# Retention and two expert layers on one core: the masks of a chunk's scores taken in the slot that computes the scores

## The chip, the cores and the metric

The kernel runs on one core of a Trainium2 chip. The metric is the device time in microseconds (us). The kernel before takes 1189.74 us, the median of three runs (1189.67 to 1189.8). The execution that the profiler recorded took 1187.96 us, 1.8 us below that median.

## The reference

A retention layer (a linear attention whose state decays by a factor per head) is followed by two feed-forward layers over 3072 tokens, d_model 512 and d_ff 2048:

```python
for t in range(S):                                   # B, H, S, D = 4, 8, 768, 64
    state = gamma * state + k[t] v[t]^T
    y[t] = scale * q[t] @ state
h = x @ w_in;  g = h - tanh(h);  x = g @ w_out       # first layer
h = x @ w_in;  g = elu(h);       x = g @ w_out       # second layer
```

The arithmetic is fp32. The kernel splits operands of its large products into a high and a low part and takes three matmuls for each product.

## The kernel before, in words

**Retention by chunks.** Each of the four sequences is cut into six chunks of 128 tokens; a step s is one chunk of one sequence (24 steps, s = 4 * chunk + sequence). For a step, TensorE (PE) computes the scores of k against q (`att_scores`, 16 records on line 164, into two PSUM banks). VectorE (DVE) multiplies both banks with a table of decays and causal zeros, which gives `pt` (line 173, two instructions: the masks), and from step 4 on multiplies q in place with a table (`att_scale_q`, line 135), which must come after the scores have read q. PE then computes the step's output (`att_out`: line 187 from the scaled q and the state, line 195 from `pt` and v) and, except in the last chunk, what the chunk adds to the state (`att_state`, line 214, from `kn`, which `att_scale_k`, line 149, has scaled on VectorE). One slot later ScalarE (ACT) copies the output into x as its high part (line 203), VectorE makes the low part (line 204), and two small VectorE instructions update the state (lines 237 and 240). The output and the first scores bank share the tag a0, the state's sum and the second scores bank share a1, so the scores of the next step wait for lines 204 and 240.

**Feed-forward by slots.** The main loop runs over slots n = 0 to 191, each one block of 512 tokens by 128 columns of d_ff. In slot n PE runs `first_mm(n)` (12 matmuls, line 251, into one of two h banks), then what `events` has for the slot, then `second_mm(n-2)` (12 matmuls, line 317, into acc). In the first layer the activation g = h - tanh(h) takes four ScalarE instructions (lines 271 to 275) and a chain of four on VectorE (lines 277, 280, 283, 284), and VectorE also makes the low part of the former slot's g (line 264).

**Weights.** They come in as 64-bit words and are converted: ScalarE writes `w32` (line 86, in the slot before), VectorE fixes the bits (lines 93 and 94), and one slot later ScalarE makes the high part (line 106) and VectorE the low one (line 107). Two weight tiles per slot are converted in slots 0 to 4, one in slots 5 to 22, none after. `w32` has four buffers, so line 86 waits until line 107 has read an older one, and ScalarE's queue stands behind it.

**Order.** Everything is under `tc.manual_schedule()`: each engine runs its instructions in the order in which the program emits them. `interleave(chain, side)` emits the activation's chain and a list of side work in turn. `events` puts the scores of steps 5 to 7 into slots 1, 3 and 5, of steps 8 to 11 into slots 22, 24, 26 and 28, and of steps 12 to 23 into slots 33 to 77; output and state of a step are in the slot after its scores. What a generator does after its `yield` runs at the head of the next slot (`for g in gens: run(g)`). `scale_k` puts line 149 at the end of the scores' slot.

Of the kernel before, what the change touches and what calls it, by code (L numbers as in the profile page):

```python
# [14 lines left out]
ALU = mybir.AluOpType  # L15
# [25 lines left out]
def retention_moe_kernel(ctx: ExitStack, tc: tile.TileContext, dims, ins, out):  # L41
    nc = tc.nc
    B, H, S, D, DM, DFF = dims
# [23 lines left out]
    dtab = const.tile([P, 2, NP, P], F32, name="dtab")  # L67
# [10 lines left out]
    def fetch(m, f):  # L78

        raw[m, f] = wp.tile([P, TB], I64, tag=f"w{m % 2}_{f}", name=f"raw{m}_{f}")  # L80
        nc.sync.dma_start(out=raw[m, f], in_=ins[f"w{m}"][f])

    def convert_a(job):

        w = w32[job] = stg.tile([P, TB], F32, tag="w32", name=f"w32_{job[0]}_{job[1]}")
        nc.scalar.activation(out=w, in_=raw[job].bitcast(F32)[:, 1::2], func=AF.Prelu, scale=REBIAS, alpha=NEG)

    def convert_b(job):

        r, w = raw[job].bitcast(U32), w32[job]  # L90
        wu = w.bitcast(U32)
        return [
            lambda: nc.vector.tensor_single_scalar(wu, wu, 3, op=ALU.logical_shift_left),
            lambda: nc.vector.scalar_tensor_tensor(
                out=wu, in0=r[:, 0::2], scalar=29, in1=wu,
                op0=ALU.logical_shift_right, op1=ALU.bitwise_or,
            ),
        ]

    def convert_c(job):  # L100

        m, f = job
        w = w32.pop(job)
        del raw[job]
        t = wts[job] = wp.tile([P, 2, TB], F32R, tag=f"w{m % 2}_{f}", name=f"w{m}_{f}")
        nc.scalar.activation(out=t[:, 0, :], in_=w, func=AF.Copy)  # L106
        return lambda: nc.vector.tensor_tensor(
            out=t[:, 1, :], in0=w, in1=t[:, 0, :].bitcast(F32), op=ALU.subtract
        )
# [7 lines left out]
    def bank(s, part):  # L117

        tag = {"sc0": "a0", "sc1": "a1", "o": "a0"}[part]
        if s < B:  # L120
            tag = [("a0", "a1", "acc0"), ("acc1", "acc2", "acc3")][s % 2][("sc0", "sc1", "o").index(part)]
        return ps_acc if tag[:3] == "acc" else ps_a, tag
# [5 lines left out]
    def att_load_v(s):  # L128
        v = att.tile([P, TB], F32, tag="v", bufs=B, name=f"v{s}")
        nc.sync.dma_start(out=v, in_=ins["qkv"][s][:, 2, :])  # L130
        qkv_t[s][1] = v

    def att_scale_q(s):
        q = qkv_t[s][0][:, 0, :].rearrange("p (a i) -> p a i", a=NP)
        nc.vector.tensor_tensor(out=q, in0=q, in1=qtab, op=ALU.mult)  # L135

    def att_load_kn(s, kn=None):
        if s // B == NCH - 1:
            return
        if kn is None:  # L140
            kn = att.tile([P, TB], F32, tag="kn", name=f"kn{s}")
        nc.sync.dma_start(out=kn, in_=ins["qkv"][s][:, 3, :])
        qkv_t[s][2] = kn

    def att_scale_k(s):
        if s // B == NCH - 1:
            return
        k = qkv_t[s][2].rearrange("p (h d) -> p h d", h=H)
        nc.vector.tensor_tensor(out=k, in0=k, in1=ktab.to_broadcast([P, H, D]), op=ALU.mult)  # L149

    def att_scores(s):
        t = qkv_t[s][0]
        if s < B:
            pt = tmp.tile([P, 2, NP, P], F32, tag="g", bufs=G_BUFS, name=f"pt{s}")
        else:
            pt = att1.tile([P, 2, NP, P], F32, tag="pt", name=f"pt{s}")
        sc = []
        for j in range(2):
            pool, tag = bank(s, f"sc{j}")
            sc.append(pool.tile([P, NP, P], F32, tag=tag, name=f"sc{s}_{j}"))  # L160
        for p in range(NP):
            for j in range(2):
                r = slice(j * D, (j + 1) * D)
                nc.tensor.matmul(
                    out=sc[j][:, p, :],
                    lhsT=t[r, 1, p * P:(p + 1) * P],
                    rhs=t[r, 0, p * P:(p + 1) * P],
                    start=True, stop=True,
                )
        pt_t[s] = pt  # L170
        yield
        for j in range(2):
            nc.vector.tensor_tensor(out=pt[:, j], in0=sc[j], in1=dtab[:, j], op=ALU.mult)  # L173
        if s >= B:
            att_scale_q(s)

    def att_out(s):
        t, v, _ = qkv_t[s]
# [66 lines left out]
    def first_mm(m, x, f, n):  # L245
        h = ps_h.tile([P, TB], F32, tag="h", name=f"h{m}_{n}")
        w = wts[m, f]
        i = 0
        for c in range(KC):
            for a, b in ((0, 0), (0, 1), (1, 0)):  # L250
                nc.tensor.matmul(  # L251
                    out=h, lhsT=w[:, a, c * P:(c + 1) * P], rhs=x[:, b, c, :],
                    start=(i == 0), stop=(i == 3 * KC - 1),
                )
                i += 1
        return h
# [6 lines left out]
    def split_lo(t, g):  # L263
        nc.vector.tensor_tensor(out=t[:, 1, :], in0=g, in1=t[:, 0, :].bitcast(F32), op=ALU.subtract)  # L264
# [107 lines left out]
    def run(g):  # L372
        for _ in g:
            pass
# [4 lines left out]
    with tc.manual_schedule():  # L379
# [36 lines left out]
        g_sc, g_out = {}, {}  # L416

        def scores_pe(s):
            g_sc[s] = att_scores(s)
            next(g_sc[s])  # L420
# [5 lines left out]
        def interleave_into(dst, lists):  # L426
            while any(lists):
                for ops in lists:
                    if ops:
                        dst.append(ops.pop(0))  # L430

        def ops(lst):
            for op in lst:
                op()
# [37 lines left out]
            run(g)  # L472
        att_load_v(B)
        att_load_kn(B)
        scores_pe(B)
        ops(convert_b(jobs0[2]))
        run(g_sc[B])
        att_scale_k(B)
        ops(convert_b(jobs0[3]))

# [15 lines left out]
        def interleave(*lists):  # L496
            while any(lists):
                for ops in lists:
                    if ops:
                        ops.pop(0)()  # L500
# [20 lines left out]
        def load_step(s):  # L521
            att_load(s, att.tile([P, 2, TB], F32, tag="qk", name=f"qk{s}"))
            att_load_kn(s)
# [6 lines left out]
        gens = []  # L530
# [6 lines left out]
        def second(upto):  # L537
            while len(pend) > upto:
                pm, pf, pn, pb, lo, hi = pend.pop(0)
                second_mm(pm, pf, pn, lo, hi)  # L540
                if pb == NB - 1 and pm == 1:
                    fetch(3, pf)
                if pf == NF - 1 and pm == 1 and pb == 0:
                    finish_rest(pb)
                elif pf == NF - 1:
                    finish(pm, pb)
                elif pf == hi - 1:
                    finish_part(pb)
# [5 lines left out]
        for ph, b, f, flo, fhi in order:  # L554
            first, last = b == 0, b == NB - 1
            for g in gens:
                run(g)
            if n < NF:
                for job in jobs0[12 + 2 * n:14 + 2 * n]:
                    fetch(*job)  # L560
            jobs = todo.get(n, [])
            h = first_mm(2 * ph, xhl[ph * NB + b], f, n)
            gens = []
            for g, *args in events.get(n, []):
                gens.append(g(*args))
                next(gens[-1], None)
            v, chain = (act_elu if ph else act_tanhshrink)(h, n, flush)
            halves = [convert_c(job) for job in prev_jobs]
            side = []
            interleave_into(side, [convert_b(j) for j in jobs])  # L570
            side += halves
            if prev_v is not None:
                side.insert(0, lambda: split_lo(g_t[n - 1], prev_v))
            interleave(chain, side)
            if n in scale_k:
                att_scale_k(scale_k[n])
            for job in todo.get(n + 1, []):
                convert_a(job)
            prev_v = v
            prev_jobs = jobs  # L580
            pend.append((2 * ph + 1, f, n, b, flo, fhi))
            if ph == 0 and last:
                fetch(2, f)
            second(SKEW)

            if n in load:
                load_step(load[n])
            if n in load_v:
                att_load_v(load_v[n])
            nxt = 0 if ph == 0 and last else b + 1 if ph else None  # L590
            if nxt is not None and nxt < NB:
                if f == 6:
                    load_x1(nxt)
                if 8 <= f < 8 + KC:
                    split_x1(nxt, f - 8)
            n += 1
# [63 lines left out]
```

## Time and profile before

| | |
|---|---|
| median of three runs | 1189.74 us |
| the profiled execution, and its span | 1187.96 us, 1186.2 us |
| PE busy | 1152.7 us, 97% of the span |
| PE weight loads busy | 943.5 us, 80% |
| VectorE busy | 682.8 us, 58% |
| ScalarE busy | 624.0 us, 53% |
| mean granted TensorE clock | 0.993 |
| chain that ended last | PE 83%, VectorE 8%, issue 4%, ScalarE 2%, DMA 2% |

A busy share is a mean over stages: VectorE's tenths in the page's 40 slices are 7 to 8 over most of the first sixth of the span and 3 to 4 in the second half. An idle time stands with the engine that waited, and what ended it with the engine that was waited for.

### The profile page before, as it was taken

How to read it: one execution, taken by the hardware profiler on the slowest of the kernel's cores; microseconds unless marked ns; L12 is line 12 of the kernel's file. 1: busy time of each engine (PE TensorE's matmuls, PEld its weight loads, DVE VectorE, ACT ScalarE, POOL GpSimd, SP SyncE). 2: the span in 40 equal slices, each digit the busy share in tenths (PEclk: the TensorE clock that was granted, in tenths of full speed). 3: DMA queues.
4: the chain of work that ended last, by engine and by line, in shares of the span. 5: the costliest groups of instructions: out<-in, count | busy, mean ns of one | idle time of the engine just before them, and what ended most of it. 6: DMA issues, size and time to landing. Idle time of an engine off the chain costs nothing.

```text
span 1186.2 us, 15678 instructions
## 1 busy us (share of the span) xinstructions
PE 1152.7 (97%) x6038; PEld 943.5 (80%) x6039; DVE 682.8 (58%) x1133; ACT 624.0 (53%) x1097; POOL 5.6 (0%) x10
## 2 busy tenths in 40 slices
PE   7799999999999999999999999999999999999998
PEld 5577887787888887888888888888888888888886
DVE  4877887656665666666689766334343333333332
ACT  2456775454445454544678766444544444453534
POOL 0000000100000000000000000000000000000000
PEclk8899999999999999999999999999999999999999
DMA  9750030513103100200476400200200200200000
GB/s 355 296 227 19 18 107 27 116 36 71 53 19 107 36 28 1 89 28 1 145 229 196 141 1 1 71 1 1 72 1 1 72 1 1 72 1 1 36 1 36
DMA packets 27562, 80.44 MB, mean 68 GB/s; under 512 B 3168, under 2 KB 3168, under 8 KB 27488
## 3 DMA queue, kind: packets, MB, share of 16 engines
q1 hardware_dynamic: 26048, 76.56, 18.6%
q0 software_dynamic: 864, 2.10, 1.2%
q8 instruction: 47, 0.77, 0.3%
q10 hardware_dynamic: 576, 0.79, 0.2%
q14 instruction: 27, 0.22, 0.1%
HBM read 64.76 MB, written 14.68 MB: 67 GB/s over the span
## 4 chain that ended last, share of the span: by engine, by line
PE 83%; DVE 8%; issue 4%; ACT 2%; DMA 2%; ACTq 0%; DVEq 0%; SPq 0%
PE acc L317 41%; PE h L251 38%; PE o L187 2%; PE o L195 2%; DVE pt L173 2%; DVE v L284 1%; DVE kn L149 1%; ACT v L272 1%; DVE v L280 1%; DVE qk L135 1%; DVE h L283 1%; DMA kn<-qkv 1%; ACT u L271 1%; DMA raw<-w 1%; DMA gtab<-gtab 1%
## 5 line engine op out<-in xcount | busy, mean ns | idle before, releaser
L317 PE MATMUL acc<-g,w 128*128 128x512 f32 x1152 | 281.8, 393 | 0.0
L251 PE MATMUL h<-x,w 128*128 128x512 f32 x1152 | 277.7, 390 | 0.0
L317 PE MATMUL acc<-w,g 128*128 128x512 f32 x1152 | 276.7, 389 | 0.6 <-DVE g L264 0.6
L251 PE MATMUL h<-y,w 128*128 128x512 f32 x1152 | 276.7, 389 | 0.0
L317 PEld LDWEIGHTS acc<-w,g 128*128 128x128 f32 x1152 | 216.2, 188 | 45.8 <-DVE g L264 1.0
L251 PEld LDWEIGHTS h<-x,w 128*128 128x128 f32 x1152 | 216.5, 188 | 45.3 <-ACT w L106 0.2
L251 PEld LDWEIGHTS h<-y,w 128*128 128x128 f32 x1152 | 216.3, 188 | 44.8
L317 PEld LDWEIGHTS acc<-g,w 128*128 128x128 f32 x1152 | 213.4, 188 | 47.0 <-ACT g L260 0.7
L297 DVE SCALAR_TENSOR_TENSOR v<-v,t 128x512 f32<-128x512 f32 x96 | 66.5, 693 | 299.6 <-ACT t L295 299.6
L292 ACT ACTIVATE u<-h 128x512 f32<-128x512 f32 x96 | 57.4, 598 | 259.8 <-PE h L251 258.3
L271 ACT ACTIVATE u<-h 128x512 f32<-128x512 f32 x96 | 57.4, 598 | 245.8 <-issue 214.5
L277 DVE SCALAR_TENSOR_TENSOR v<-v,u 128x512 f32<-128x512 f32 x96 | 66.4, 692 | 161.4 <-ACT v L272 161.3
L264 DVE TENSOR_TENSOR g<-v,g 128x512 fp32r<-128x512 f32 x192 | 131.5, 685 | 0.8 <-ACT g L260 0.8
L260 ACT ACTIVATE g<-v 128x512 fp32r<-128x512 f32 x192 | 118.1, 615 | 2.0 <-DVE v L300 2.0
L284 DVE COPY_PREDICATED v<-m,h 128x512 f32<-128x512 uint16 x96 | 70.7, 736 | 6.0
L272 ACT ACTIVATE v<-u,qa_b 128x512 f32<-128x512 f32 x96 | 69.5, 724 | 3.2
L275 ACT ACTIVATE m<-u,xs_b 128x512 bf16<-128x512 f32 x96 | 68.2, 710 | 0.0
L283 DVE TENSOR_TENSOR h<-h,t 128x512 f32<-128x512 f32 x96 | 66.5, 693 | 0.0
L300 DVE TENSOR_TENSOR v<-h,v 128x512 f32<-128x512 f32 x96 | 65.7, 684 | 0.0
L280 DVE SCALAR_TENSOR_TENSOR v<-v,h 128x512 f32<-128x512 f32 x96 | 65.3, 681 | 0.0
L293 ACT ACTIVATE v<-u 128x512 f32<-128x512 f32 x96 | 60.6, 631 | 3.1
L295 ACT ACTIVATE t<-u 128x512 f32<-128x512 f32 x96 | 59.2, 617 | 0.0
(44 smaller groups left out, 605.2 us busy)
## 6 DMA issues: line engine op xcount, KB each, us to landing
raw<-w SPq DMA_DIRECT2D x64, 512.0 KB, 5.4
qk<-qkv SPq DMA_DIRECT2D x20, 512.0 KB, 4.7
v<-qkv SPq DMA_DIRECT2D x24, 256.0 KB, 6.1
x<-x1d SPq DMA_DIRECT2D x12, 512.0 KB, 5.8
kn<-qkv SPq DMA_DIRECT2D x20, 256.0 KB, 5.6
out<-o SPq DMA_DIRECT2D x10, 512.0 KB, 2.9
x1d<-o SPq DMA_DIRECT2D x8, 512.0 KB, 3.4
stage<-qkv SPq DMA_DIRECT2D x4, 512.0 KB, 6.8
```

What stands on the lines that cost most here:

```text
L251: nc.tensor.matmul(out=h, lhsT=w[:, a, c * P:(c + 1) * P], rhs=x[:, b, c, :], start=(i == 0), stop=(i == 3 * KC - 1),)
L260: nc.scalar.activation(out=t[:, 0, :], in_=g, func=AF.Copy)
L264: nc.vector.tensor_tensor(out=t[:, 1, :], in0=g, in1=t[:, 0, :].bitcast(F32), op=ALU.subtract)
L271: nc.scalar.activation(out=u, in_=h, func=AF.Square)
L272: nc.scalar.activation(out=v, in_=u, func=AF.Square, bias=qa_b)
L275: nc.scalar.activation(out=big, in_=u, func=AF.Relu, bias=xs_b)
L277: lambda: nc.vector.scalar_tensor_tensor(out=v, in0=v, scalar=QB, in1=u, op0=ALU.add, op1=ALU.mult),
L280: lambda: nc.vector.scalar_tensor_tensor(out=v, in0=v, scalar=C2, in1=h, op0=ALU.mult, op1=ALU.mult),
L283: lambda: nc.vector.tensor_tensor(out=h, in0=h, in1=th, op=ALU.subtract),
L284: lambda: nc.vector.copy_predicated(out=v, mask=big.bitcast(U16), data=h),
L297: lambda: nc.vector.scalar_tensor_tensor(out=v, in0=v, scalar=1.0, in1=th, op0=ALU.add, op1=ALU.mult),
L317: nc.tensor.matmul(out=acc[e], lhsT=lhsT, rhs=rhs, start=(f == lo and i == 0), stop=(f == hi - 1 and i == 2),)
```

## The change

The masks and the scaling of q of step 5 and later are no longer run at the head of the slot after the scores. `att_scores` hands them out as three functions at its `yield`; the main loop puts them into the side list of the scores' own slot, behind its first entry, so that they alternate with the activation's chain. Steps 0 to 3 keep their order, and step 4's is the same as before.

```diff
         pt_t[s] = pt
-        yield
-        for j in range(2):
-            nc.vector.tensor_tensor(out=pt[:, j], in0=sc[j], in1=dtab[:, j], op=ALU.mult)
-        if s >= B:
-            att_scale_q(s)
+        masks = [
+            lambda j=j: nc.vector.tensor_tensor(out=pt[:, j], in0=sc[j], in1=dtab[:, j], op=ALU.mult)
+            for j in range(2)
+        ]
+        if s < B:
+            yield
+            for op in masks:
+                op()
+        else:
+            yield masks + [lambda: att_scale_q(s)]
...
             gens = []
+            masks = []
             for g, *args in events.get(n, []):
                 gens.append(g(*args))
-                next(gens[-1], None)
+                masks += next(gens[-1], None) or []
...
             if prev_v is not None:
                 side.insert(0, lambda: split_lo(g_t[n - 1], prev_v))
+            side[1:1] = masks
             interleave(chain, side)
```

Only VectorE's order changes; that of PE, ScalarE, SyncE and GpSimd is the same. In the rows below `v` and `h` are the activation's chain, `w` the weights, `pt` the masks' results, `sc` the scores, `qk` the scaling of q and `kn` that of k. Line numbers of the changed kernel are up to five higher, and the masks' line is 172.

VectorE in slot 1 (scores of step 5), from behind line 280 of the chain, before:

```order
L93 TENSOR_SCALAR w_0_4_433<-w_0_4_433 128x512
L283 TENSOR_TENSOR h_1_447<-h_1_447,t_472 128x512
L93 TENSOR_SCALAR w_1_2_435<-w_1_2_435 128x512
L284 COPY_PREDICATED v_473<-m_474,h_1_447 128x512
L94 SCALAR_TENSOR_TENSOR w_0_4_433<-raw_4_155,w_0_4_433 128x512
L94 SCALAR_TENSOR_TENSOR w_1_2_435<-raw_2_157,w_1_2_435 128x512
L107 TENSOR_TENSOR w_3_481<-w_0_3_359,w_3_481 128x512
L107 TENSOR_TENSOR w_1_483<-w_1_1_361,w_1_483 128x512
L149 TENSOR_TENSOR kn_365<-kn_365,ktab 128x512
L173 TENSOR_TENSOR pt_460<-sc_0_461,dtab 128x512
L173 TENSOR_TENSOR pt_460<-sc_1_462,dtab 128x512
L135 TENSOR_TENSOR qk_363<-qk_363,qtab 128x512
```

and now:

```order
L172 TENSOR_TENSOR pt_460<-sc_0_461,dtab 128x512
L288 TENSOR_TENSOR h_1_447<-h_1_447,t_472 128x512
L172 TENSOR_TENSOR pt_460<-sc_1_462,dtab 128x512
L289 COPY_PREDICATED v_473<-m_474,h_1_447 128x512
L135 TENSOR_TENSOR qk_363<-qk_363,qtab 128x512
L93 TENSOR_SCALAR w_0_4_433<-w_0_4_433 128x512
L93 TENSOR_SCALAR w_1_2_435<-w_1_2_435 128x512
L94 SCALAR_TENSOR_TENSOR w_0_4_433<-raw_4_155,w_0_4_433 128x512
L94 SCALAR_TENSOR_TENSOR w_1_2_435<-raw_2_157,w_1_2_435 128x512
L107 TENSOR_TENSOR w_3_481<-w_0_3_359,w_3_481 128x512
L107 TENSOR_TENSOR w_1_483<-w_1_1_361,w_1_483 128x512
L149 TENSOR_TENSOR kn_365<-kn_365,ktab 128x512
```

The three instructions move ahead of six instructions on weights and of the scaling of k, which all come three places later.

VectorE in slot 24 (scores of step 9, no weights any more), before:

```order
L280 SCALAR_TENSOR_TENSOR v_1834<-v_1834,h_24_1808 128x512
L283 TENSOR_TENSOR h_24_1808<-h_24_1808,t_1833 128x512
L284 COPY_PREDICATED v_1834<-m_1835,h_24_1808 128x512
L149 TENSOR_TENSOR kn_1727<-kn_1727,ktab 128x512
L173 TENSOR_TENSOR pt_1821<-sc_0_1822,dtab 128x512
L173 TENSOR_TENSOR pt_1821<-sc_1_1823,dtab 128x512
L135 TENSOR_TENSOR qk_1725<-qk_1725,qtab 128x512
```

and now:

```order
L285 SCALAR_TENSOR_TENSOR v_1834<-v_1834,h_24_1808 128x512
L172 TENSOR_TENSOR pt_1821<-sc_0_1822,dtab 128x512
L288 TENSOR_TENSOR h_24_1808<-h_24_1808,t_1833 128x512
L172 TENSOR_TENSOR pt_1821<-sc_1_1823,dtab 128x512
L289 COPY_PREDICATED v_1834<-m_1835,h_24_1808 128x512
L135 TENSOR_TENSOR qk_1728<-qk_1728,qtab 128x512
L149 TENSOR_TENSOR kn_1730<-kn_1730,ktab 128x512
```

The scaling of q passes the scaling of k, and both masks stand between instructions of the chain.

## Rows read from the trace of the kernel before

**Rows 1.** Waits of PE: who waited for whom, total us, times, longest us.

```profile
PE o L187 <- DVE qk L135: 16.2, 15, 2.9
```

**Rows 2.** Busy time by stretch: start:end, us, PE, PEld, DVE, ACT, POOL busy, PE clock, DMA share, GB/s.

```profile
71.00:76.00 5.00, 2.87 (x28) 2.57 (x30) 5.00 (x11) 4.14 (x8) 0.00 (x0) 0.74 1.02 419
...
112.00:178.00 66.00, 66.00 (x293) 54.67 (x292) 55.73 (x97) 52.55 (x95) 0.00 (x0) 1.00 0.19 65
178.00:244.00 66.00, 62.52 (x460) 50.58 (x459) 47.48 (x80) 31.71 (x56) 3.69 (x4) 1.00 0.32 80
244.00:460.00 216.00, 211.48 (x1301) 172.72 (x1300) 136.50 (x221) 104.70 (x181) 1.74 (x2) 1.00 0.15 43
```

**Rows 3.** PE in order of time: starts of outputs; start us, us long, [idle before <- releaser].

```profile
73.13 1.75 PE L187 MATMUL o<-qk,st 64*64 64x128 f32 x16 [2.81 <-DVE qk L135]
92.20 1.09 PE L187 MATMUL o<-qk,st 64*64 64x128 f32 x16 [2.45 <-DVE qk L135]
190.71 1.09 PE L187 MATMUL o<-qk,st 64*64 64x128 f32 x16 [1.90 <-DVE qk L135]
206.28 1.09 PE L187 MATMUL o<-qk,st 64*64 64x128 f32 x16 [0.56 <-DVE qk L135]
```

**Rows 4.** Slot 24 in order of time (the columns of rows 3).

```profile
201.64 0.68 DVE L280 SCALAR_TENSOR_TENSOR v<-v,h 128x512 f32<-128x512 f32 x1
202.83 2.88 PE L251 MATMUL h<-x,w 128*128 128x512 f32 x12
203.66 0.67 DVE L149 TENSOR_TENSOR kn<-kn,ktab 128x512 f32<-128x512 f32 x1
204.25 1.28 DVE L173 TENSOR_TENSOR pt<-sc,dtab 128x512 f32<-128x512 f32 x2
205.45 0.68 DVE L135 TENSOR_TENSOR qk<-qk,qtab 128x512 f32<-128x512 f32 x1
```

**Rows 5.** Slots 1 and 2 in order of time.

```profile
45.28 2.93 PE L164 MATMUL sc<-qk 64*128 64x128 f32 x16 [4.77 <-DVE x L204]
47.20 0.68 DVE L280 SCALAR_TENSOR_TENSOR v<-v,h 128x512 f32<-128x512 f32 x1
50.88 1.29 DVE L107 TENSOR_TENSOR w<-w,w 128x512 fp32r<-128x512 f32 x2
51.60 1.27 ACT L86 ACTIVATE w<-raw 128x512 f32<-128x512 f32 x2 [3.21 <-DVE w L107]
54.49 0.69 DVE L277 SCALAR_TENSOR_TENSOR v<-v,u 128x512 f32<-128x512 f32 x1
```

**Rows 6.** The page's groups: line engine op out<-in xcount | busy, mean ns | idle before.

```profile
L271 ACT ACTIVATE u<-h 128x512 f32<-128x512 f32 x96 | 57.4, 598 | 245.8 <-issue 214.5
...
L272 ACT ACTIVATE v<-u,qa_b 128x512 f32<-128x512 f32 x96 | 69.5, 724 | 3.2
```

**Rows 7.** Slots 3 to 6 in order of time.

```profile
61.88 0.69 DVE L204 TENSOR_TENSOR x<-o,x 128x512 fp32r<-128x512 f32 x1 [1.21 <-ACT x L203]
62.91 1.74 PE L164 MATMUL sc<-qk 64*128 64x128 f32 x16
64.39 0.69 DVE L277 SCALAR_TENSOR_TENSOR v<-v,u 128x512 f32<-128x512 f32 x1 [0.96 <-ACT v L272]
...
79.69 0.69 DVE L204 TENSOR_TENSOR x<-o,x 128x512 fp32r<-128x512 f32 x1 [0.63 <-ACT x L203]
82.92 1.16 PE L164 MATMUL sc<-qk 64*128 64x128 f32 x16
94.71 3.02 PE L317 MATMUL acc<-g,w 128*128 128x512 f32 x12
```

**Rows 8.** Slots 22 and 23 in order of time.

```profile
184.73 0.68 DVE L280 SCALAR_TENSOR_TENSOR v<-v,h 128x512 f32<-128x512 f32 x1
185.93 2.88 PE L251 MATMUL h<-x,w 128*128 128x512 f32 x12
...
192.66 0.63 PE L214 MATMUL ds<-v,kn 128*64 128x64 f32 x16
```

More of the change, by code (lines that the diff above doesn't have):

```diff
@@ L474, in retention_moe_kernel @@
         att_load_kn(B)
-        scores_pe(B)
+        masks4 = next(att_scores(B))
         ops(convert_b(jobs0[2]))
-        run(g_sc[B])
+        ops(masks4)
         att_scale_k(B)
```

## The prediction, as put on record before the changed kernel had run

> **What bounds the kernel now.** The page's engine shares come first: PE is busy 97% of the span, so the time is PE's work plus the little that PE waits. The second view is the list of PE's waits, and one line of it belongs to this change: PE's output matmuls on line 187 wait 15 times for VectorE's scaling of q on line 135, 16.2 us in all, at most 2.9 [rows 1]. The third view, busy time by stretch, says where. From 178 to 244 us PE is idle for 66 - 62.52 = 3.48 us, from 244 to 460 us for 216 - 211.48 = 4.52, and from 112 to 178 us not at all [rows 2]. The fourth, PE in order of time, splits this: 2.81 and 2.45 us in slots 4 and 6, 1.90 in slot 23 and 0.56 in slot 25 [rows 3]. So there are three kinds: three waits in slots 2, 4 and 6, together 16.2 - 3.48 - 4.52 = 8.2 us; one of 1.90 in slot 23; and eleven more, 3.48 - 1.90 + 4.52 = 6.1 us together, some 0.56 each. The four outputs of the last chunk are the remaining ones of the 19; there k isn't scaled, and they don't wait.
>
> The change adds and removes no instruction. It moves three VectorE instructions per step, for 19 steps; PE, ScalarE and both DMA-issuing queues keep their order. So each kind is laid out anew with its own rows.
>
> **The eleven late waits.** In slot 24 the chain's line 280 starts at 201.64, and then come lines 283, 284, 149, the two masks and line 135, which ends at 205.45 + 0.68 = 206.13; PE starts the output 0.15 later, though `first_mm` had ended at 202.83 + 2.88 = 205.71 [rows 3, 4]. Two masks follow each other within 1.20 us while they take 1.28 together, so independent instructions start 0.60 apart [rows 4]. Now five starts lie between line 280 and the scaling of q: it starts at 201.64 + 5 x 0.60 = 204.64, ends at 205.32, and PE may go at 205.47, 0.24 before it gets there. The wait goes whole. What is late next is the scaling of k, which ends about 0.6 later at 205.9; the state matmuls need it only 192.66 - 190.71 = 1.95 us behind the output's start [rows 3, 8], so it is covered. The chain's last instruction is up to 1.2 us later; the next slot's ScalarE work on it comes behind two other instructions of 0.60 and 0.72 us [rows 6] that themselves wait for the next h, and PE uses it two slots on: nothing. **Minus 6.1.**
>
> The Trainium skill (VectorE: DVE Perf Modes, "The DRAIN you can't avoid") says that the next VectorE instruction does not start until the pipe has emptied. The two masks overlap by 0.08 us here, so the trace doesn't agree for these; by that rule the sum would be that of rival three.
>
> **Slot 23.** Line 280 starts at 184.73 [rows 8]. The scaling of q now ends at 184.73 + 3.0 + 0.68 = 188.4, and with 0.15 PE may go at 188.6; `first_mm` ends at 185.93 + 2.88 = 188.81. The output starts 1.9 us earlier. Behind the scaling of q there now stand one weight's three instructions and the scaling of k. At 0.60 each that is 187.7 + 4 x 0.60 = 190.1 for the start of the latter and 190.9 until PE sees it; the state is due at 188.81 + 1.95 = 190.8. 0.1 comes back. **Minus 1.8.**
>
> **Slots 1 to 6.** Here VectorE is the shorter side: it is busy 5.00 of 5.00 us from 71 to 76 [rows 2], and the three moved instructions now stand ahead of the weights. In slot 1 line 280 starts at 47.20, so the first mask could start at 47.8, but the scores end only at 45.28 + 2.93 = 48.2 [rows 5]: VectorE, an in-order queue, stands for 0.4 with the chain behind it. The weights' line 107 comes 3 x 0.60 + 0.4 = 2.2 later, at 53.1 instead of 50.88. ScalarE's line 86 waits for it (it starts 0.72 behind it), takes 1.27, then u takes 0.60 and v 0.72 [rows 5, 6]: the chain of slot 2 starts at 53.1 + 3.3 = 56.4, 1.9 later than its 54.49. In the kernel before the masks filled this gap; now little does. So line 204, which frees the scores' bank, starts at 61.88 + 1.9 = 63.8, and the scores of step 6, at 62.91 without a wait before, start at 63.8 + 0.69 + 0.1 = 64.6 [rows 7]. The 2.9 us won at the output of slot 2 (part of which goes to waiting for k) are lost here, and 1.7 more.
>
> In slot 3 the chain started at 64.39 and now starts behind the late lines 204, 237 and 240, at about 65.2. With 0.8 of lateness and 1.8 for the three instructions the weights are 2.6 late, and the chain of slot 4, by the same 3.3 us, about 2.3. Bounds: 1.9 if slot 3 adds nothing to what slot 1 left, 3.7 if its three instructions add whole; I take 2.3, nearer to the first, since slot 3's own chain is only 0.8 late. Line 204 of slot 5 is then at 79.69 + 2.3 = 82.0, and the scores of step 7 start at 82.8 (82.92 before) and take 1.74 as those at 62.91 did, since their second bank waits for line 240 again [rows 7]. PE goes on at 84.5; `second_mm` and `first_mm`, 2.88 each [rows 4], end at 90.3; the output no longer waits; output and state take 94.71 - 92.20 = 2.5 [rows 3, 7]. `second_mm(4)` starts at 92.8 instead of 94.71. **Minus 1.9** (2.3 and 0.5 at the bounds): of 8.2 us most only changes its name, from a wait for q to one for line 204. From there PE has no wait until 178 [rows 2], and the gain is carried on.
>
> **The sum.** 1.9 + 1.8 + 6.1 = 9.8 us off the profiled execution's 1187.96 gives 1178.2; that execution lies 1.8 below the median of the runs, so on their scale 1189.74 - 9.8 = **1179.9 us**.
>
> **The rivals.** *One: TensorE's clock falls at the new pauses.* Before the scores of steps 6 and 7 PE now stands for some 2 to 4.5 us (1.7 late, and PE is there up to 2.9 early). A pause of 4.77 us before 45.28 was followed by scores of 2.93 us, where 1.16 is usual; one of 2.81 before 73.13 by a mean granted clock of 0.74 in that stretch, a mixture of 2.4 and 1.2 GHz; one of 2.45 before 92.20 by nothing [rows 2, 3, 5, 7]. If both new pauses cost 2.93 - 1.16 = 1.8, the early part is 3.6 - 1.9 = 1.7 slower and the total 6.2 faster: 1183.5. Against it: PE is ahead of VectorE there, which hides part, and two old pauses go. The Trainium skill (TensorE: Matmul & The Clock Gate, "HAM oscillation — how this bites in real kernels") has waits re-throttling the array; the row at 45.28 agrees.
>
> *Two: nothing comes back.* All 16.2 us go: 1173.5. For it: the three instructions are moved, not added, so VectorE has no more to do. Against it: ScalarE's line 86 waits 3.21 us for line 107 as it is [rows 5], and now line 107 comes later.
>
> *Three: an interleaved instruction costs its whole duration.* Five starts of 0.69 put the scaling of q at 205.09 and PE at 205.92, 0.21 behind `first_mm`. Each late wait shrinks by 0.35 instead of 0.56, eleven times 3.8 us: minus 7.5, 1182.2. Against it stands the 0.60 of rows 4.
>
> *Four, on the other side: the weights' loop passes every delay on.* VectorE waits for ScalarE, and ScalarE's line 86 for VectorE. If in each of the three early pairs the 2.2 us of slot 1 land whole on PE beyond today's waits, each with a clock loss of 1.8, the early part is 3 x 4.0 = 12.0 slower, and 12.0 - 7.9 = 4.1 gives 1193.8. It decides once a pair loses over 2.6 us. Against it: PE's 8.2 us of waiting absorb the first such delays, and slot 5 converts a single weight.
>
> **The numbers.** The forecast has 0.68, rivals one to four 0.12, 0.07, 0.07 and 0.03, and no visible effect 0.03. The range goes from 1176.0 (the forecast with early slots that give back half of the 6.3 us, 1176.7, rounded down) to 1184.5 (rival one, rival three, and the 1.8 us by which the runs and the profiled execution differ, in part). 0.2%, about what a measurement tells from no change, is 2.4 us. Faster by more: 0.94, within it 0.03, slower 0.03.
>
> **What would show it.** In PE's list line 187 should no longer wait for line 135; from 244 to 460 us PE's idle time should fall from 4.5 us to nearly nothing, and the output of slot 25 should start with `first_mm`'s end. In the early slots the wait should stand on line 164 for lines 204 and 240, some 2 to 4 us at steps 6 and 7 each, and ScalarE's line 86 should wait longer than 3.21. Waits of about 0.2 left on line 135 would speak for rival three, granted clocks well below 1 between 60 and 90 us for rival one, and a time above 1187.4 would make the forecast wrong.

## The result and the profile after

The changed kernel takes 1177.55 us (median of four executions, 1177.25 to 1178.54) against 1189.77 before (median of four, 1189.67 to 1191.4): a ratio of 0.9896, 95% interval 0.9878 to 0.9913, 12.2 us less. Two pairs of numbers have to be kept apart. The executions with a trace are 1187.96 before and 1178.54 after, 9.4 us apart. The traced execution of before is among the shortest of its kernel (the fifteen beside the first four experiments went from 1187.25 to 1191.61) and lies 1.8 us under its median; after's is the longest of its four, 1.0 over its median. The traces explain the 9.4 us; the experiments bear on the other 2.8.

The list of PE's waits after, in the columns of [rows 1]:

```profile
PE sc L164 <- DVE x L209: 8.6, 3, 4.8
PE sc L164 <- DMA stage<-qkv: 2.8, 3, 2.1
PE o L200 <- DVE pt L172: 2.0, 4, 1.2
...
PE sc L164 <- DVE st L245: 0.7, 2, 0.4
```

The 16.2 us on the scaling of q are gone, all fifteen. What has grown is the line on the scores: 4.8 us before, once, now 8.6 in three times. The line of before:

```profile
PE sc L164 <- DVE x L204: 4.8, 1, 4.8
```

ScalarE's line 86 of slot 1, which waited 3.21 us for line 107 before [rows 5], now waits longer, as the prediction had it:

```profile
53.46 1.28 ACT L86 ACTIVATE w<-raw 128x512 f32<-128x512 f32 x2 [5.06 <-DVE w L107]
```

Busy time by stretch shows the late part without a gap, where [rows 2] had 3.48 and 4.52 us:

```profile
66.00:71.00 5.00, 5.00 (x19) 3.94 (x16) 5.00 (x10) 1.28 (x3) 0.00 (x0) 0.50 1.02 418
...
175.00:240.00 65.00, 65.00 (x472) 52.60 (x471) 48.80 (x83) 32.88 (x57) 3.69 (x4) 1.00 0.33 82
240.00:455.00 215.00, 215.00 (x1319) 175.82 (x1318) 135.91 (x222) 106.21 (x184) 1.74 (x2) 1.00 0.15 44
```

In the first of these rows TensorE has half its clock (0.50, 1.2 GHz). In the same stretch of before it had all of it:

```profile
66.00:71.00 5.00, 4.32 (x19) 3.21 (x18) 5.00 (x10) 2.00 (x4) 0.00 (x0) 1.00 1.02 419
```

Slot 24 in order of time, to be read beside [rows 4]:

```profile
199.15 0.68 DVE L285 SCALAR_TENSOR_TENSOR v<-v,h 128x512 f32<-128x512 f32 x1
199.75 0.68 DVE L172 TENSOR_TENSOR pt<-sc,dtab 128x512 f32<-128x512 f32 x1
200.35 2.88 PE L256 MATMUL h<-x,w 128*128 128x512 f32 x12
200.35 0.69 DVE L288 TENSOR_TENSOR h<-h,t 128x512 f32<-128x512 f32 x1
200.95 0.68 DVE L172 TENSOR_TENSOR pt<-sc,dtab 128x512 f32<-128x512 f32 x1
201.55 0.73 DVE L289 COPY_PREDICATED v<-m,h 128x512 f32<-128x512 uint16 x1
202.16 0.68 DVE L135 TENSOR_TENSOR qk<-qk,qtab 128x512 f32<-128x512 f32 x1
202.76 0.69 DVE L149 TENSOR_TENSOR kn<-kn,ktab 128x512 f32<-128x512 f32 x1
203.16 1.09 PE L192 MATMUL o<-qk,st 64*64 64x128 f32 x16
```

The starts are 0.60 apart throughout, and the scaling of q has ended at 202.84 when PE comes to the output at 203.16.

### The profile page after: what moved, and what is told of

It is laid out like the page before. It is cut to its first block, busy times and chain, and to the rows that moved or that the text cites. A ratio compares the mean times of both kernels' runs of the same rounds, so it can differ in the third digit from the quotient of the medians.

```text
span 1176.7 us, 15687 instructions
## 1 busy us (share of the span) xinstructions
PE 1154.5 (98%) x6039; PEld 943.2 (80%) x6039; DVE 681.3 (58%) x1133; ACT 623.9 (53%) x1097; POOL 5.6 (0%) x10
## 4 chain that ended last, share of the span: by engine, by line
PE 93%; DVE 3%; DMA 2%; ACT 1%; issue 1%; ACTq 0%; SPq 0%; DVEq 0%
PE acc L322 45%; PE h L256 43%; PE sc L164 2%; PE o L200 1%; PE o L192 1%; DMA kn<-qkv 1%; DMA raw<-w 1%; DMA gtab<-gtab 1%; PE ds L219 1%; DVE w L94 0%; DVE w L107 0%; DVE x L209 0%; DVE pt L172 0%; DVE v L289 0%; ACT w L86 0%
```

## Where the 9.4 us of the two traces come from

| stretch | before | after | difference |
|---|---|---|---|
| to the scores of step 8 (start) | 181.98 | 181.29 | -0.7 |
| from there to the scores of step 9 (slot 23) | 16.90 | 15.11 | -1.8 |
| from there to the scores of step 20 (eleven late waits) | 274.64 | 267.80 | -6.8 |

The three differences make 9.3 us; nearly nothing is left for what follows. The starts of the scores in the trace after, which give the right column (before: 181.98, 198.88 and 473.52):

```profile
181.29 1.16 PE L164 MATMUL sc<-qk 64*128 64x128 f32 x16
...
196.40 1.16 PE L164 MATMUL sc<-qk 64*128 64x128 f32 x16
...
464.20 1.16 PE L164 MATMUL sc<-qk 64*128 64x128 f32 x16
```

## The experiments

Each ran beside the kernel before on the same chip, and each edit is made to the changed kernel. Every expectation sets a theory A against a rival. "Under before" is counted from the median of before in the same set: 1189.78 in the first four, 1189.31 in the next four, 1189.47 in the last two.

**1. The early slots alone.**

```diff
-        if s < B:
+        if s < B or s >= 2 * B:
             yield
             for op in masks:
                 op()
+            if s >= B:
+                att_scale_q(s)
```

> Only steps 5 to 7 (slots 1, 3 and 5) take masks and scaling of q in the scores' slot; steps 8 to 23 do it at the head of the next slot, as before. Theory A (three parts that add up; early most of the gain is given back at the scores): 0.7 to 2 us under the kernel before, 1187.7 to 1189.0. Rival (the early slots hold what the medians show beyond the late waits, 12.2 - 8.6): 3.6 us under it, 1186.1. In the trace both have PE waiting on line 164 for line 204, about 3 us at step 6, and the eleven waits of about 0.56 still there.

Measured: 1187.61 (eleven executions, 1186.07 to 1189.06), 2.2 us under before, ratio 0.9985 (0.9976 to 0.9994). That is just below theory A's range, and the interval leaves the rival's 3.6 out. The early wait on the scores is there (8.4 us in three), and so are the eleven late waits and the 1.90 of slot 23. In this trace TensorE's clock falls at that wait, which the traced execution of before did not show:

```profile
179.81 1.16 PE L164 MATMUL sc<-qk 64*128 64x128 f32 x16
...
188.53 1.64 PE L194 MATMUL o<-qk,st 64*64 64x128 f32 x16 [1.90 <-DVE qk L135]
190.10 1.97 PE L202 MATMUL o<-pt,v 128*64 128x128 f32 x16
...
198.35 1.16 PE L164 MATMUL sc<-qk 64*128 64x128 f32 x16
```

The output matmuls take 1.64 and 1.97 us instead of 1.09 and 1.09: from the scores of step 8 to those of step 9 it takes 198.35 - 179.81 = 18.54 us instead of 16.90.

**2. The late slots alone** (the same edit with `B < s < 2 * B`).

> Only steps 8 to 23 are changed, the early three are as before. Theory A: 11 x 0.62 + 1.8 = 8.6 us under the kernel before, 1181.1, early waits of 2.9, 2.8 and 2.5 for line 135 still there. Rival (nearly all of the gain is late, the early slots are even): 10 to 12 us under it, 1178 to 1180.

Measured: 1179.55 (1179.4 to 1179.81), 10.2 us under before, ratio 0.9919 (0.9905 to 0.9933). By the medians the rival's number is right; by the trace theory A's is: 15.11 us from step 8 to 9 and 465.10 - 197.29 = 267.81 from 9 to 20, the same as in the changed kernel, 8.6 us less than the trace of before. So the late part is 8.6 us of waits, and by the medians about 1.6 more; the interval, 8.0 to 11.3 us, holds both numbers. The two parts alone make 2.2 + 10.2 = 12.4, the whole change 12.2: they add up.

**3. Not interleaved, only put ahead of the scaling of k.**

```diff
-            side[1:1] = masks
             interleave(chain, side)
+            for op in masks:
+                op()
             if n in scale_k:
                 att_scale_k(scale_k[n])
```

> Masks and scaling of q are not interleaved but stand at the end of the scores' slot, behind the activation and the weights and ahead of the scaling of k; against the kernel before only the scaling of k has changed its place. Theory A (a late wait is the 0.60 of the scaling of k that stood ahead): all eleven late waits go, since the scaling of q then ends at 205.54 of the old trace against the 205.71 at which PE is there; slot 23 and the three early waits shrink by 0.6 each: 11 x 0.6 + 0.6 + 1.8 = 9.0 us under the kernel before, 1180.7. Rival (it takes the interleaving to hide them): waits of 0.3 or more stay, 4 to 6 us under it, 1184 to 1186.

Measured: 1177.84 (1177.73 to 1177.95), ratio 0.9904 (0.9889 to 0.9919), as fast as the changed kernel. PE's waits, and from the trace the output of step 8 (slot 23), the scores of step 9 and its output (slot 25):

```profile
PE o L192 <- DVE qk L135: 5.5, 4, 1.6
PE sc L164 <- DVE x L209: 5.0, 2, 4.7
```

```profile
187.11 1.09 PE L192 MATMUL o<-qk,st 64*64 64x128 f32 x16 [1.30 <-DVE qk L135]
195.33 1.16 PE L164 MATMUL sc<-qk 64*128 64x128 f32 x16
202.12 1.09 PE L192 MATMUL o<-qk,st 64*64 64x128 f32 x16
```

All eleven late waits are gone without any interleaving: the 0.6 us of the scaling of k was the whole of them. Slot 23's wait shrank by 0.60 as forecast, the early three from 2.9, 2.8 and 2.5 to 1.29, 1.64 and 1.25, by 1.6, 1.2 and 1.2 where 0.6 each was forecast. The median is 2.9 us better than the 9.0 forecast; in the trace the early slots had won 181.98 - 178.98 = 3.0 us by the scores of step 8, where 1.8 was laid out. Why they shrank by that much isn't shown.

**4. The scaling of k ahead of the scaling of q, in the changed kernel.**

```diff
+            if n in scale_k:
+                masks.insert(2, lambda: att_scale_k(scale_k[n]))
             side[1:1] = masks
             interleave(chain, side)
-            if n in scale_k:
-                att_scale_k(scale_k[n])
```

> The changed kernel with one instruction moved: the scaling of k is interleaved ahead of the scaling of q, so 0.60 more stands before it. Theory A (margin of 0.24 us before PE gets there): 0.36 of each late wait comes back, eleven times 4.0 us, and about 0.4 in slot 23; 1177.6 + 4.4 = 1182.0. Rival (the wait went because the instructions alternate, not because of their place): no wait comes back, 1177.6.

Measured: 1183.55 (1183.31 to 1185.5), ratio 0.9955 (0.9943 to 0.9967), 6.0 us slower than the changed kernel where 4.4 was forecast (5.1 by the two traces). The waits come back at the size that was laid out, ten of 0.36, one of 0.26, and one of 0.36 in slot 23:

```profile
PE o L192 <- DVE qk L135: 4.2, 12, 0.4
```

```profile
188.75 1.09 PE L192 MATMUL o<-qk,st 64*64 64x128 f32 x16 [0.36 <-DVE qk L135]
...
196.93 1.16 PE L164 MATMUL sc<-qk 64*128 64x128 f32 x16
204.12 1.09 PE L192 MATMUL o<-qk,st 64*64 64x128 f32 x16 [0.36 <-DVE qk L135]
...
469.31 1.16 PE L164 MATMUL sc<-qk 64*128 64x128 f32 x16
```

From step 9 to step 20 it takes 469.31 - 196.93 = 272.38 us, 4.58 more than in the changed kernel, or 0.42 for each of the eleven, most of which read 0.36. So place decides, not alternation; and a wait costs 0.06 more than its row says.

**5 and 6. Step 8 alone changed, and all but step 8** (the edit of experiment 1 with `s > B and s != 2 * B`, and with `s == 2 * B`).

> Only step 8 is changed (scores in slot 22, output in slot 23, the one wait of 1.90 us); everything else as before. Theory A (that wait is worth 1.8 and also lowers TensorE's clock in a part of the executions, which the profiled one of before didn't show: in the run with the early slots alone its output took 1.64 us instead of 1.09): 3.0 to 3.5 us under the median before, 1186.5, and the executions lie closer together than the 4.4 us (1187.25 to 1191.61) of before. Rival (the clock there plays no part): 1.8 under it, 1188.0, spread as before.

> The changed kernel with step 8 alone as before. Theory A: 1.8 plus 1 to 1.6 us above the changed kernel's 1177.6 in the median, about 1180.7, and executions spread over 1.5 us or more, with the wait of 1.9 us on line 135 back. Rival: 1179.4, executions within 1 us of each other as in the changed kernel.

All but step 8: 1181.55 median, 4.0 us above the changed kernel's 1177.55; four of five executions between 1181.23 and 1181.91, one at 1179.27. That looks like two levels, the rival's 1179.4 once and one about 2 us above it four times; the mean granted clock recorded with each execution parts them in the same way, 0.994 for the one and 0.991 for the four. The trace is of the upper level. Its scores of steps 8 and 9:

```profile
181.37 1.16 PE L164 MATMUL sc<-qk 64*128 64x128 f32 x16
...
199.83 1.16 PE L164 MATMUL sc<-qk 64*128 64x128 f32 x16
```

Stretches of it around slot 23, and then the same stretches of the trace of before, in which the clock didn't fall there (columns of [rows 2]):

```profile
186.00:190.00 4.00, 2.19 (x10) 1.50 (x8) 4.00 (x8) 1.69 (x3) 0.00 (x0) 1.00 0.00 0
190.00:194.00 4.00, 3.90 (x49) 3.65 (x49) 3.92 (x7) 2.37 (x5) 0.00 (x0) 0.64 0.34 125
194.00:198.00 4.00, 4.00 (x17) 3.30 (x18) 1.22 (x3) 0.00 (x0) 0.00 (x0) 0.93 0.22 76
```

```profile
186.00:190.00 4.00, 2.81 (x13) 2.00 (x11) 4.00 (x8) 1.07 (x2) 0.00 (x0) 1.00 0.00 0
190.00:194.00 4.00, 3.29 (x51) 2.97 (x52) 3.92 (x7) 2.98 (x6) 0.00 (x0) 1.00 0.22 60
194.00:198.00 4.00, 4.00 (x19) 3.30 (x18) 1.82 (x4) 0.00 (x0) 0.00 (x0) 1.00 0.38 140
```

The same wait of 1.90 us is followed by a granted clock of 0.64 in one and 1.00 in the other; from step 8 to 9 it takes 199.83 - 181.37 = 18.46 us in the one, 16.90 in the other. The fall costs 1.6.

Step 8 alone: 1187.79, only 1.5 us under before (ratio 0.9986, 0.9977 to 0.9995). Theory A's 3.0 to 3.5 missed, outside the interval, and the rival's 1.8 is right in the median; the executions do lie closer together, 1186.64 to 1188.46 where before has 1187.18 to 1191.72 in the same set. In its trace slot 23 is at full clock and without a wait, but the scores of step 8 start at 183.65, 1.7 later than in the trace of before. That is lost behind the output of step 7, where both wait 2.45 us:

```profile
92.31 1.09 PE L194 MATMUL o<-qk,st 64*64 64x128 f32 x16 [2.45 <-DVE qk L135]
...
99.24 2.88 PE L258 MATMUL h<-x,w 128*128 128x512 f32 x12
```

Between these two starts lie 6.93 us, in the trace of before 97.57 - 92.20 = 5.37. So the clock can fall behind an early pause too. How often it falls at which pause can't be told from one trace per kernel.

**7 to 9. Other orders for the early slots.** Experiment 7 takes the third experiment's order for steps 5 to 7 and the change's for the rest. Experiment 8 is the change with ScalarE's copy of the output ahead of line 86, experiment 9 both.

```diff
-            side[1:1] = masks
+            if n > 5:
+                side[1:1] = masks
+                masks = []
             interleave(chain, side)
+            for op in masks:
+                op()
...
+            if n in (0, 2, 4):
+                for g in gens:
+                    run(g)
+                gens = []
             for job in todo.get(n + 1, []):
                 convert_a(job)
```

> Steps 5 to 7 with masks and scaling of q at the slot's end, ahead of the scaling of k (as in the third experiment), steps 8 to 23 as in the changed kernel. Theory A (the stretches add up; in the early slots the masks are better spent filling the time in which ScalarE works on the next weights, with the scores of step 6 waiting 0.2 us instead of 3.05): the third experiment's early slots were 2.3 us ahead of the changed kernel's and its slot 23 1.3 behind: 1177.8 - 1.4 = 1176.4, 1.2 us under the changed kernel. Rival (what the early slots win there is lost again by slot 22): 1177.6.

> The changed kernel, with ScalarE's copy of the output (line 208) ahead of the two conversions on line 86 in slots 0, 2 and 4, and VectorE's lines 209, 242 and 245 with it at the end of that slot. Theory A (the scores of steps 5, 6 and 7 wait for line 209 only because line 208 stands behind line 86, which waits for line 107): each pause gets about 1.2 us shorter (4.8 to 3.5, 3.0 to 1.8, 0.8 to 0), the next chain starts 0.7 earlier each time, about 2 us in all: 1175.5. Rival (VectorE's total work there decides, the pauses only move): 1177.5, with new waits for line 135 or 149 in their place.

> The order of the seventh experiment (steps 5 to 7 at the slot's end, the rest interleaved) together with the eighth's early output copy. Theory A (the early gains are of two kinds, less waiting for line 135 and an earlier release of the scores' bank, and add up in part): the pause before the scores of step 5 gets 1.2 us shorter, its chain starts 0.7 earlier, the later pauses were gone already: 0.7 to 1.0 us under the seventh's 1175.9, about 1175.0. Rival (VectorE's work in slots 1 to 6 sets the end): 1175.9 as either alone.

Seven: 1175.86 (1175.05 to 1176.15), ratio 0.9885 (0.9867 to 0.9903), 1.7 under the changed kernel where 1.2 was forecast. Eight: 1176.03 (1173.91 to 1176.74), ratio 0.9886 (0.9869 to 0.9903), 1.5 under it where 2.0 was; its pauses before the scores became 3.44, 1.74 and none, as laid out, and a wait of 1.43 before the state matmuls of step 5 is new (the list of waits names nothing that it waited for). Nine does not add up: 1176.78 (1174.6 to 1178.16), ratio 0.9895 (0.9878 to 0.9913). With the scores earlier and the masks still last, PE waits longer at the outputs, 2.78 us in slot 4 instead of seven's 1.61, and TensorE's clock falls behind it; the rival's 1175.9, VectorE's work setting the end, is nearer than theory A's 1175.0. The intervals of seven and eight overlap the change's; the four executions of seven are all below the lowest of the eight of the changed kernel (1176.39), the only sign that it is a better order, by about 0.1%.

**10. The changed kernel again.**

> The changed kernel once more, for how far its executions lie apart beside kernels with a wait in slot 23. Theory A (spread comes from TensorE's clock falling or not at a pause, and the changed kernel's early pauses are left): median 1177.3 to 1178.0, executions within 1.5 us, all far from the 4.5 us of the kernel before. Rival (the narrow spread of the first four was chance): a spread of 3 us or more.

Measured: 1177.13 (1176.39 to 1177.2), ratio 0.9900 (0.9885 to 0.9915); the spread is 0.8 us, as theory A had it, the median 0.2 below its range. Its trace differs from the first one's mainly in one place. The scores of step 6 and what follows, in the first trace and then in this one:

```profile
64.17 0.48 PE L164 MATMUL sc<-qk 64*128 64x128 f32 x2 [3.05 <-DVE x L209]
65.03 2.07 PE L164 MATMUL sc<-qk 64*128 64x128 f32 x14 [0.38 <-DVE st L245]
67.03 5.17 PE L322 MATMUL acc<-g,w 128*128 128x512 f32 x12
...
74.85 1.09 PE L192 MATMUL o<-qk,st 64*64 64x128 f32 x16
...
94.02 3.02 PE L322 MATMUL acc<-g,w 128*128 128x512 f32 x12
```

```profile
64.28 0.49 PE L164 MATMUL sc<-qk 64*128 64x128 f32 x2 [3.00 <-DVE x L209]
65.14 1.54 PE L164 MATMUL sc<-qk 64*128 64x128 f32 x14 [0.37 <-DVE st L245]
66.61 4.22 PE L322 MATMUL acc<-g,w 128*128 128x512 f32 x12
...
73.48 1.09 PE L192 MATMUL o<-qk,st 64*64 64x128 f32 x16
...
92.67 3.02 PE L322 MATMUL acc<-g,w 128*128 128x512 f32 x12
```

The pause is the same, 3.0 us, and the clock falls behind both, but for longer in the first: its `second_mm` takes 5.17 us against 4.22, and its `second_mm(4)` starts 1.35 us later.

## Why the prediction was right, and what was off

The forecast was 1179.9 in a range of 1176.0 to 1184.5; 1177.55 is in it, 2.4 us below. By its own steps:

- **The eleven late waits** (6.1): right in the mechanism, sized too small: 6.8. Experiments 3 and 4 show that the place ahead of the scaling of k was the cause and that 0.60 us decides. What mis-sized the term is the step "`first_mm` had ended at 202.83 + 2.88". Where nothing waits, the next matmul starts 2.81 behind `first_mm`'s start (200.35 and 203.16 above), inside its recorded end. A row's idle time so misses 0.06 to 0.07 us of each wait, 0.7 us over the eleven.
- **Rival three**, that an alternating instruction costs its whole duration, fell: the starts are 0.60 apart. The rule named beside it (the Trainium skill, VectorE: DVE Perf Modes, "The DRAIN you can't avoid") doesn't describe these independent instructions; the same section adds that a next instruction that is not held starts earlier, and the 0.60 between starts of instructions 0.68 long fits that.
- **Slot 23** (1.8): 1.79 in the trace, a little by luck. The output is 1.97 us earlier against the scores of step 8 (1.9 laid out), and 0.18 of it is given back by the scores of step 9 (0.1 laid out); the two misses cancel. By medians the wait was worth 4.0 us in experiment 6, where the clock fell behind it (1.79 and 1.6 are shown by the traces, the rest isn't), and 1.5 in experiment 5.
- **Slots 1 to 6** (1.9, bounds 0.5 and 2.3): the mechanism is the one laid out. The chain of slot 2 starts late (56.02, 56.4 forecast), line 209 frees the scores' bank late, the scores of step 6 start at 64.17 (64.6 forecast) and those of step 7 at 83.91 and 82.53 in the two traces (82.8). `second_mm(4)` starts at 94.02 and 92.67 (92.8): 0.7 and 2.0 won, 0.7 where rival one came true in part. Its price was 1.8 us per pause. At step 6 the scores and `second_mm` take 3.1 and 1.6 us longer than at full clock in the two traces; at step 7 the pause was only 0.8 us, not the 2 to 4 that were expected, and no fall followed. The ground put against the rival, that PE is ahead there and hides part, isn't borne out: of the 1.5 us by which the two traces differ at step 6, 1.35 are still there at `second_mm(4)`, and the wait before the scores of step 7 is 0.8 in both.
- **The scale of the runs.** The step "on their scale 1189.74 - 9.8" is where most of the 2.4 us were lost. It took the 1.8 us between the traced execution and the median for a constant. The runs point to the clock behind the waits: the traces of experiments 1 and 6 hold a fall at slot 23 that the trace of before lacks, and the change removes the wait and the fall. Of before's other executions none has a trace, but 37 of them have a recorded mean granted clock: the eight at 0.994 have a median of 1188.2 us, the thirteen at 0.993 one of 1189.5, the eleven at 0.991 one of 1189.9 and the five at 0.990 or less one of 1191.6. So before's longer executions had less clock; that they lost it at slot 23 is argued, and experiment 5, where it was lost behind step 7 instead, shows that slot 23 isn't the only place. Nor does less clock always cost time: the changed kernel's shortest of the first four has 0.991, the other three 0.993 or 0.994. The rival on the clock was priced only at pauses that the change makes; that two old pauses go stood beside it without a price.

Rivals two (all 16.2 us) and four (slower) did not come: of the early 8.2 us, 0.7 to 2.0 stayed won.

## What to carry to other kernels

A consumer that waits a fraction of a microsecond for the last of several short instructions may need no more than another order among them: first what the consumer needs now, then what it needs 2 us later. Where the producing engine has no time to spare, as in the early slots here, the same move only gives the wait another name, and one should follow the chain to the engine that refills it. A removed wait can be worth more than its own length where the clock fell behind it in some executions, as in experiment 6, though not in experiment 5. Take the time from several executions: a trace may lie at either end of them.

## What the runs showed of the hardware that was not expected

The same pause is followed by different granted clocks in different executions: in the changed kernel, behind the 3.0 us before the scores of step 6, it was 0.50 from 66 to 71 us in the first trace and 0.68 in that of experiment 10. Behind a wait of 1.90 us it stayed at 1.00 in the trace of before and was 0.64 over the next 4 us in experiment 6. The kernel of experiment 6, with that one wait, spread over 2.6 us in five executions; without it the changed kernel's two sets spread over 1.3 and 0.8 us and the second experiment over 0.4. But experiments 8 and 9, which don't have it either, spread over 2.8 and 3.6, so the spread alone doesn't tell at which pause the clock fell. And a wait of 0.36 us on PE costs 0.42, one of 0.56 costs 0.62, since PE's recorded ends lie about 0.07 behind the point at which the next matmul can start (2.88 us recorded for `first_mm`, 2.81 to the next start where nothing waits).
